# A fused attention and expert kernel on one core: the unused general path made smaller, and the written-out order of the main path replaced

## The chip, the cores and the metric

The kernel runs on one core of a Trainium2 chip. The metric is device time in microseconds, the median of three runs: 174.09 us before the change (173.5 to 175.12). Lower is better. The engines are named as in the profile: PE multiplies matrices, ACT and DVE evict results and do element-wise work, POOL does more element-wise work, SP issues nearly all transfers.

## The reference, cut to what matters

Four batches of 11,456 tokens with 128 channels each. In each batch 32 inducing points attend to all tokens, then every token attends to the 32 results (h). The outcome goes through a router with eight experts, of which each token takes one.

```python
def mab(q, kv):
    s = scale * (q @ kv.transpose(0, 2, 1))
    s = s - s.max(-1, keepdims=True)
    a = np.exp(s)
    a /= a.sum(-1, keepdims=True) + 1e-09
    return a @ kv
h = mab(I, x)
return mab(x, h).astype(np.float32)
...
expert_idx = np.argmax(logits, axis=1)
...
for e in range(E):
    mask = expert_idx == e
    h = np.maximum(x[mask] @ w1[e], 0.0)
    out[mask] = gate_w[mask, None] * (h @ w2[e])
```

## The kernel before, in words

Each batch is cut into six tiles of 1,920 tokens (the last is shorter), 24 tiles in all, numbered g = 0 to 23; tiles 0 to 5 are batch 0, 6 to 11 batch 1, and so on.

The first pass over a tile is `load g` (SP brings 960 KB with channels on partitions into one of ten xT buffers), `s1 g` (scores on PE), `e1 g` (exponentials on ACT), `e1t g` (transposed by DVE) and `h g` (PE accumulates). For `h` the tile is needed with tokens on partitions as well: for the 12 tiles in `LOADED` SP loads that form too (`loadx g`, 960 KB into one of two xD buffers), for the others PE transposes it (`xt g`) and ACT or DVE evicts it (`xe g`). When a batch's six tiles are in, `finish` makes the batch's tables: `hsb`, `hd`, `hdc`, `tab`, then `pick` takes one expert for the whole batch, and `loadw` fetches that expert's two weight matrices (2 x 512 KB), which are read first by `G b` on PE.

The second pass over a tile is `s2 g` (scores against h, the last reader of the tile, after which its xT buffer is free for another load), `e2`, `ud`, `w`, then by pairs of tiles a chain of small steps (`n2`, `ln`, `ex`, `fac`, `den`, `lg`, `el`, `S`, `v`, `gf`), then `F`, `eg`, `out g` on PE, two evictions `oe g.0` and `oe g.1`, and `store g` on SP.

Every such step is one named operation. The string `ORDER` lists all 855 of them; each engine does its own in the order of that string and waits for what they depend on. `BY_DVE` names those done by DVE rather than by their first engine. `Plan.run` walks through `ORDER` with assumed durations (`LATENCY`, `LATE`, `LEAVE` and others are its constants); what it works out decides which buffer of a kind a step takes and where a few dummy matmuls (line 777) are put in. SP's queue goes in order: a load that waits for a free buffer holds back the stores behind it. At most `DEPTH` = 6 loads are under way.

At the end `verdict` (DVE) sums up checks on the shortcuts taken: one int, `ni`, the number of batches for which they did not hold. All five engines read it (line 818, `nc.values_load`) and enter a loop over that many batches (line 821), which computes a batch in a general way, expert by expert. With these inputs `ni` is 0, so the loop's body is never run: each engine loads the value, branches past the body, waits for the outstanding stores, and leaves.

## Time and profile before

| what | before |
|---|---|
| time, median of 3 runs (range) | 174.09 us (173.5 to 175.12) |
| the profiled execution's own time | 173.58 us |
| its span, first to last instruction | 171.8 us |
| PE busy | 154.9 us, 90% of the span |
| DVE, ACT, POOL busy | 123.3, 112.8, 62.7 us |
| moved by DMA | 62.92 MB on SP's queue |
| granted TensorE clock, mean | 0.97 |

Time and span differ by 1.8 us, which lies before the first and after the last instruction. The chain of work that ended last ends at 161.4 us with the verdict; the rest of the span up to 171.8 us is the way out of the program.

### The profile page before, as it was taken

The page shows a single profiled execution, that of the slowest core. Times are in us where ns is not written, and L with a number is a line of the kernel's source. Part 1 is how long each engine was busy: PE and PEld are TensorE (multiplying, and loading weights), DVE is VectorE, ACT ScalarE, POOL GpSimd, SP SyncE. Part 2 cuts the span into 40 slices and gives each one's busy share as a digit, 9 for nine tenths or more (in the row PEclk, how much of TensorE's full clock was granted, in tenths as well). Part 3 has the DMA queues.
Part 4 walks back from the last instruction along what each step waited for, and adds up shares of the span by engine and source line. Part 5 has one row for each costly group of instructions (what it writes and reads, how often), then busy time and mean ns, then how long its engine had stood idle before and what let it go on. Part 6 is the DMA issues. An engine that isn't in the chain of part 4 may idle for free.

```text
span 171.8 us, 5945 instructions
## 1 busy us (share of the span) xinstructions
PE 154.9 (90%) x2383; PEld 84.2 (49%) x2383; DVE 123.3 (72%) x318; ACT 112.8 (66%) x240; POOL 62.7 (37%) x164
## 2 busy tenths in 40 slices
PE   7999999999999999879979999999999999998200
PEld 5686974238955325447257443545733233655100
DVE  0444183887887999668968688898879989988400
ACT  2086923648936798578645975888969899876300
POOL 8400001074126524613133531853650475946000
PEclk9999999999999999999999999999999999999855
DMA  5999999999999589999999999999978999779920
GB/s 171 433 424 411 420 413 419 406 395 423 398 422 415 175 254 422 419 423 424 419 419 418 417 415 420 417 417 420 415 304 334 337 419 396 309 316 391 399 104 8
DMA packets 10865, 63.38 MB, mean 369 GB/s; under 512 B 1352, under 2 KB 1360, under 8 KB 10832
## 3 DMA queue, kind: packets, MB, share of 16 engines
q1 hardware_dynamic: 10656, 62.92, 91.0%
q8 instruction: 21, 0.34, 0.8%
q14 instruction: 12, 0.10, 0.2%
q10 hardware_dynamic: 176, 0.02, 0.1%
HBM read 39.47 MB, written 23.46 MB: 366 GB/s over the span
## 4 chain that ended last, share of the span: by engine, by line
PE 77%; DMA 12%; DVE 3%; issue 1%; SPq 0%; DVEq 0%
PE psum L344 59%; PE psum L448 10%; PE psum L777 7%; DMA w<-in_w 7%; DMA xD<-in_xP 6%; PE psum L416 1%; DVE o L341 1%; PE psum L705 0%; DVE Wp L613 0%; DVE E1T L474 0%; DVE am L595 0%; DVE fl L708 0%; SPq L517 0%; DVE hsb L341 0%; DVE ei L512 0%
## 5 line engine op out<-in xcount | busy, mean ns | idle before, releaser
L341 ACT COPY o<-psum 128x960 f32<-128x960 f32 (+2 forms) x48 | 39.7, 849 | 9.4 <-PE psum L344 8.2
L676 POOL TENSOR_TENSOR E2g<-E,F 128x480 f32<-128x480 f32 (+2 forms) x26 | 26.5, 1031 | 17.5 <-PE psum L344 8.4
L344 PE MATMUL psum<-E2g,K 32*128 32x480 f32 (+2 forms) x232 | 27.1, 542 | 0.5 <-DVE Wp L613 0.2
L344 PE MATMUL psum<-xT,ind 128*32 128x480 f32 x192 | 24.8, 572 | 0.7 <-DMA xT<-in_xT 0.7
L474 DVE STREAM_TRANSPOSE E1T<-E 128x480 f32<-128x480 f32 x24 | 16.0, 670 | 12.1 <-PE psum L344 8.0
L341 ACT COPY xP<-psum 128x1024 f32<-128x1024 f32 (+1 forms) x19 | 18.1, 965 | 8.8 <-PE psum L448 8.8
L448 PEld LDWEIGHTS psum<-ident,xT 128*128 128x128 f32 x180 | 19.8, 142 | 5.3 <-issue 1.6
L344 PE MATMUL psum<-xT,hd 128*32 128x480 f32 x192 | 22.4, 569 | 0.0
L344 PE MATMUL psum<-E,tab 32*32 32x480 f32 x192 | 22.0, 567 | 0.1
L344 PE MATMUL psum<-E,tD 32*32 32x480 f32 x192 | 22.0, 567 | 0.0
L448 PE MATMUL psum<-ident,xT 128*128 128x128 f32 x180 | 21.9, 277 | 0.1
L465 ACT ACTIVATE E<-psum,nb 128x480 f32<-128x480 f32 x24 | 15.8, 659 | 7.7 <-PE psum L344 6.2
L599 ACT ACTIVATE E<-psum,nb 128x480 f32<-128x480 f32 x24 | 14.8, 660 | 5.2 <-DVE nb L419 3.2
L595 DVE TENSOR_REDUCE am<-psum 128x1 f32<-128x480 f32 x24 | 15.3, 648 | 2.0 <-PE psum L344 1.6
L613 POOL TENSOR_TENSOR Wp<-U,E 128x480 f32<-128x480 f32 x9 | 10.9, 1210 | 15.0 <-ACT U L341 14.8
L674 DVE STREAM_TRANSPOSE F<-gf 128x480 f32<-128x480 f32 (+2 forms) x29 | 16.1, 570 | 0.3
L344 PEld LDWEIGHTS psum<-E2g,K 32*128 32x128 f32 x232 | 9.3, 183 | 11.8 <-issue 6.5
L777 PE MATMUL psum<-zero 128*128 128x256 bf16 x82 | 13.1, 306 | 1.3 <-DVE zero L301 1.1
L344 PE MATMUL psum<-xD,E1T 128*32 128x128 f32 x360 | 13.0, 274 | 1.3 <-DMA xD<-in_xP 1.3
L635 DVE TRANSPOSE_TENSOR_REDUCE n<-Wp 128x30 f32<-128x960 f32 x12 | 13.8, 1154 | 0.2
L344 PEld LDWEIGHTS psum<-xD,E1T 128*32 128x32 f32 x360 | 11.0, 110 | 5.7 <-DMA xD<-in_xP 3.2
L344 PE MATMUL psum<-xP,E1T 128*32 128x128 f32 x360 | 13.4, 274 | 0.1
(139 smaller groups left out, 212.2 us busy)
## 6 DMA issues: line engine op xcount, KB each, us to landing
xT<-in_xT SPq DMA_DIRECT2D x19, 960.0 KB, 10.6
out<-o SPq DMA_DIRECT2D x17, 960.0 KB, 9.3
xD<-in_xP SPq DMA_DIRECT2D x12, 960.0 KB, 9.7
w<-in_w SPq DMA_DIRECT2D x8, 512.0 KB, 9.2
xT<-in_xT SPq DMA_DIRECT2D x4, 928.0 KB, 13.5
out<-o SPq DMA_DIRECT2D x5, 512.0 KB, 3.1
out<-o SPq DMA_DIRECT2D x2, 928.0 KB, 5.8
out<-o SPq DMA_DIRECT2D x3, 448.0 KB, 3.5
```

Of the source, the lines that this page charges most:

```text
L341: return nc.scalar.copy(out, in_) if e == "ACT" else ENG[e].tensor_copy(out, in_)
L344: return nc.tensor.matmul(out, lhsT=lhsT, rhs=rhs, start=start, stop=stop)
L448: return [nc.tensor.transpose(ap(tp)[:, (q - q0) // 4, 128 * ((q - q0) % 4):128 * ((q - q0) % 4) + 128], v(q), ident) for q in range(q0, q1)]
L465: return [nc.scalar.activation(ap(e1), ap(ps)[:, :W], AF.Exp, bias=bt.t("nb")[:, 0:1], scale=SCALE, accum_out=bt.t("zk")[:, k:k + 1])]
L474: add(f"e1t {g}", {"DVE": 0.59}, lambda e: [nc.vector.transpose(ap(e1t), ap(e1))], [e1], [e1t])
L595: add(f"am {g}", {"DVE": 0.57}, lambda e, ps=ps, k=k: [v.tensor_reduce(t("am")[:, k:k + 1], ap(ps)[:, :W], AX.X, ALU.max, apply_absolute_v ...
L599: add(f"e2 {g}", {"ACT": 0.56}, lambda e, ps=ps, a=a: [nc.scalar.activation(ap(e2)[:, a], ap(ps)[:, :W], AF.Exp, bias=t("nb")[:, 1:2], sca ...
L613: return [ENG[e].tensor_tensor(ap(wp)[:, a], src(), ap(e2)[:, a], ALU.mult)]
L635: add("n2 " + nm, {"DVE": 1.08}, lambda e: [v.tensor_reduce(fl2(u("n2")), ap(wp).rearrange("p a (q i) -> p (a q) i", i=32), AX.X, ALU.add, ...
L674: add(f"F {nm}", {"DVE": 0.09 + 0.51 * part}, lambda e, a=a, f=f, q0=q0, q1=q1: [v.transpose(ap(f).rearrange("p (q i) -> p q i", i=32)[:, ...
L676: add(f"eg {nm}", {"POOL": 0.06 + 1.15 * part, "DVE": 0.2 + 0.54 * part}, lambda e, a=a, f=f, e2g=e2g, c0=c0, c1=c1: [ENG[e].tensor_tensor ...
L777: fill = [nc.tensor.matmul(psum[:, s, 0:256], lhsT=zero[:, 0:P], rhs=zero, start=True, stop=True) for _ in range(n)]
```

## The change

Three things are changed. First, the body of the general path handles 64 tokens at a time where it handled 358 in three blocks, and its experts are a loop where they were written out eight times: the body's matmuls in the program go from 179 to 28, of which the expert part's go from 128 to 16. Second, `ORDER` and `BY_DVE` are replaced; the operations are the same 855, 32 became 34 of them on DVE, `LOADED` and `W_POOL` stay. Third, `Plan.run` holds every user of a buffer until the buffer is free, where it held only the first; and two of its constants are other (`LATE`, `LEAVE`).

```diff
-ORDER = """load 0.1, ind, load 0.0, load 1, xt 0.1, xe 0.1, s1 0, m1 0, small, en1, xt 0.0, xe 0.0, sha 0, shb 0, s1 1,
+ORDER = """load 0.1, xt 0.1, small, xe 0.1, ind, load 0.0, s1 0, m1 0, xt 0.0, xe 0.0, sha 0, load 1, s1 1, shb 0, shc 0,
...
-    LAND, LATE = 1.2, 0.5
-    LEAVE = 4.0
+    LAND, LATE = 1.2, 1.2
+    LEAVE = 3.0
...
-                    if self.since[b.kind][s] > 0:
-                        t = max(t, self.since[b.kind][s] + wait)
+                    b.open = max(b.open, self.since[b.kind][s])
             for b in o.bufs:
+                if b.open > 0:
+                    t = max(t, b.open + wait)
...
-    GW = 358
-    BLK = ((0, 128), (128, 128), (256, 102))
+    GW = 64
...
-            for e in range(E):
-                nc.sync.dma_start(wr, w1[e])
-                nc.sync.dma_start(w2p, w2[e])
+            with tc.For_i(0, E, 1) as e:
+                nc.sync.dma_start(wr, w1[bass.ds(e, 1)].rearrange("o c f -> (o c) f"))
+                nc.sync.dma_start(w2p, w2[bass.ds(e, 1)].rearrange("o p h c -> (o p) h c"))
+                v.tensor_tensor(r2, place, at_e, ALU.is_equal)
+                v.tensor_scalar_add(at_e, at_e, -1.0)
+                v.tensor_scalar(sq, y, r2, r1, ALU.mult, ALU.mult)
+                nc.tensor.transpose(bank[6][:, 0:GW], sq, ident[:GW, :GW])
+                v.tensor_copy(yg, bank[6][:, 0:GW])
                 for f in range(8):
-                    mm(bank[f % 2][:, :GW], wr[:, P * f:P * f + P], yg[:, e])
-                    nc.scalar.activation(hid, bank[f % 2][:, :GW], AF.Relu)
-                    mm(bank[7][:, :GW], w2p[:, f], hid, start=e == 0 and f == 0, stop=e == E - 1 and f == 7)
-            v.tensor_copy(ot, bank[7][:, :GW])
+                    mm(bank[0][:, :GW], wr[:, P * f:P * f + P], yg)
+                    nc.scalar.activation(hid, bank[0][:, :GW], AF.Relu)
+                    mm(bank[7][:, :GW], w2p[:, f], hid, start=f == 0, stop=f == 7)
+                v.tensor_tensor(ot, ot, bank[7][:, :GW], ALU.add)
```

What the new order does at three places is shown by the instructions as they stand on an engine. `xT_n`, `xD_n` and `xP_n` are buffers of a tile, not tile numbers; the tiles are named in the sentences. Line numbers after the change are one higher.

SP, the first loads, before: tiles 3, 4 and 5, then the second form of tile 3 (`loadx 3`), then tile 6.

```order
L433 DMA xT_68<-in_xT 128x1920
L433 DMA xT_69<-in_xT 128x1920
L433 DMA xT_70<-in_xT 128x1856
L440 DMA xD_78<-in_xP 128x1920
L433 DMA xT_71<-in_xT 128x1920
```

After:

```order
L434 DMA xT_68<-in_xT 128x1920
L434 DMA xT_70<-in_xT 128x1920
L434 DMA xT_69<-in_xT 128x1856
L434 DMA xT_71<-in_xT 128x1920
L441 DMA xD_78<-in_xP 128x1920
```

`load 6` and `loadx 3` have changed places.

SP, in the middle of batch 1, before: loads of tiles 15 and 16, `loadx 13`, `load 17` (which takes the buffer that tile 6 leaves), `store 0`, `load 13`, `store 1`, and the read of the expert's number ahead of `loadw 1`.

```order
L433 DMA xT_68<-in_xT 128x1920
L433 DMA xT_69<-in_xT 128x1920
L440 DMA xD_79<-in_xP 128x1920
L433 DMA xT_71<-in_xT 128x1856
L689 DMA out<-o_97 128x1920
L433 DMA xT_72<-in_xT 128x1920
L689 DMA out<-o_98 128x1920
L517 TENSOR_LOAD ei
```

After: `loadx 13`, `load 13`, `loadx 14`, `load 15`, `store 0`, `load 18` (into the buffer that tile 6 leaves), `store 1`, loads of tiles 16, 20 and 17, the read ahead of `loadw 1`.

```order
L441 DMA xD_78<-in_xP 128x1920
L434 DMA xT_70<-in_xT 128x1920
L441 DMA xD_79<-in_xP 128x1920
L434 DMA xT_69<-in_xT 128x1920
L690 DMA out<-o_97 128x1920
L434 DMA xT_71<-in_xT 128x1920
L690 DMA out<-o_98 128x1920
L434 DMA xT_72<-in_xT 128x1920
L434 DMA xT_73<-in_xT 128x1920
L434 DMA xT_67<-in_xT 128x1856
L518 TENSOR_LOAD ei
```

`store 0` now stands ahead of the load that takes tile 6's buffer, and `load 13` well ahead of it. Between that load and `loadw 1` stand `store 1` and three loads, where `store 0`, `load 13` and `store 1` stood.

PE, where batch 1's weights are first read (`G 1`, the row with `w_149`), before: `s1 13`, `s1 16`, `h 12`, `G 1`, `s2 10`, `s2 11`, `h 13`.

```order
L344 MATMUL psum<-xT_72,ind 32x480 x4
L344 MATMUL psum<-xT_69,ind 32x480 x4
L344 MATMUL psum<-xP_76,E1T_82 32x128 x15
L344 MATMUL psum<-w_149,hd_127 32x256 x4
L344 MATMUL psum<-xT_65,hd_127 32x480 x4
L344 MATMUL psum<-xT_66,hd_127 32x480 x4
L344 MATMUL psum<-xD_79,E1T_82 32x128 x15
```

After, from `s1 13` on, and then from the transposes of tile 17 (23 rows further down) to `h 15`:

```order
L345 MATMUL psum<-xT_70,ind 32x480 x4
L345 MATMUL psum<-xP_75,E1T_83 32x128 x15
L345 MATMUL psum<-xT_65,hd_127 32x480 x4
L345 MATMUL psum<-xT_74,hd_127 32x480 x4
L345 MATMUL psum<-xD_78,E1T_83 32x128 x15
```

```order
L449 MATMUL psum<-ident,xT_67 128x128 x15
L345 MATMUL psum<-w_149,hd_127 32x256 x4
L345 MATMUL psum<-E2g_95,K_122 128x480 x4
L345 MATMUL psum<-xT_67,ind 32x480 x4
L345 MATMUL psum<-xT_71,ind 32x480 x4
L706 MATMUL psum<-ident,chk_123 6x128
L345 MATMUL psum<-tD_129,ones 32x8 x4
L345 MATMUL psum<-ad_164,ones 32x8 x4
L345 MATMUL psum<-xD_78,E1T_83 32x128 x15
```

`G 1` has moved from behind `h 12` to behind the transposes of tile 17, past `s2 11`, `s2 10`, `h 13`, `s1 15`, `h 14`, `out 2`, `ud 10` and `ud 11` (`s1 16` stays ahead of it); and `s1 18`, the transpose for `ck2 0` and the two steps of `md 1` now stand ahead of `h 15` (the last row).

## Rows read from the trace of the kernel before

**Rows 1.** The profile's page: PE's line of the busy times, then the DMA engines' busy share and rate in 40 equal slices of 4.3 us.

```profile
PE 154.9 (90%) x2383; PEld 84.2 (49%) x2383; DVE 123.3 (72%) x318; ACT 112.8 (66%) x240; POOL 62.7 (37%) x164
...
DMA  5999999999999589999999999999978999779920
GB/s 171 433 424 411 420 413 419 406 395 423 398 422 415 175 254 422 419 423 424 419 419 418 417 415 420 417 417 420 415 304 334 337 419 396 309 316 391 399 104 8
```

**Rows 2.** The page's DMA queues: packets, MB, share of the 16 engines' span.

```profile
q1 hardware_dynamic: 10656, 62.92, 91.0%
q8 instruction: 21, 0.34, 0.8%
```

**Rows 3.** Busy time of the engines by stretch (PE, PEld, DVE, ACT, POOL), granted clock, DMA share and rate.

```profile
56.00:64.00 8.00, 8.00 (x116) 2.68 (x114) 7.20 (x23) 6.91 (x17) 3.65 (x6) 1.00 0.69 200
...
124.00:138.00 14.00, 13.78 (x196) 4.64 (x185) 12.26 (x38) 11.35 (x21) 5.70 (x10) 1.00 0.87 333
```

**Rows 4.** PE's own busy time by stretch, with granted clock, DMA share and rate.

```profile
4.90:69.80 64.90, 64.70 (x1043) 1.00 0.98 389
69.80:87.10 17.30, 14.37 (x229) 1.00 1.02 419
87.10:147.80 60.70, 60.27 (x972) 1.00 0.97 392
```

**Rows 5.** PE's instructions in order of time at its three waits for transfers between 64 and 92 us (start, duration; idle time before in brackets): `s1 13` with `s1 16`, `G 1`, `h 15`.

```profile
70.45 1.82 PE L344 MATMUL psum<-xT,ind 128*32 128x480 f32 x16 [0.67 <-DMA xT<-in_xT]
...
74.06 0.64 PE L344 MATMUL psum<-w,hd 128*32 128x256 f32 x8 [0.93 <-DMA w<-in_w]
...
87.08 1.07 PE L344 MATMUL psum<-xD,E1T 128*32 128x128 f32 x30 [1.30 <-DMA xD<-in_xP]
```

**Rows 6.** SP's issues in order of time: `load 17`, `store 0`, `load 13`, `loadw 1`; and, from SP's waits between 40 and 70 us, that of `load 17`.

```profile
58.85 0.33 SPq L433 DMA_DIRECT2D xT<-in_xT  x1
59.22 0.43 SPq L689 DMA_DIRECT2D out<-o  x1
59.75 0.38 SPq L433 DMA_DIRECT2D xT<-in_xT  x1
...
62.57 0.34 SPq L519 DMA_DIRECT2D w<-in_w  x1
...
SPq L433 <- PE psum L344: 9.0, 1, 9.0
```

**Rows 7.** ACT in order of time: the second of the two evictions of tile 0's output (`oe 0.0`).

```profile
55.36 0.97 ACT L341 COPY o<-psum 128x960 f32<-128x960 f32 x1
```

**Rows 8.** The first `loadx` and its user: SP's issue of `loadx 3`, its time to landing (last column), and `h 3` on PE.

```profile
5.72 0.33 SPq L440 DMA_DIRECT2D xD<-in_xP  x1
...
xD<-in_xP SPq DMA_DIRECT2D x1, 960.0 KB, 14.9
...
22.15 1.22 PE L344 MATMUL psum<-xD,E1T 128*32 128x128 f32 x30
```

**Rows 9.** The two issues of `loadw 2` with KB each and time to landing; then SP's issues of `store 6` and `loadw 2` in order of time, and `G 2` on PE.

```profile
w<-in_w SPq DMA_DIRECT2D x2, 512.0 KB, 9.2
...
98.52 0.38 SPq L689 DMA_DIRECT2D out<-o  x1
100.65 0.35 SPq L519 DMA_DIRECT2D w<-in_w  x1
...
111.01 0.62 PE L344 MATMUL psum<-w,hd 128*32 128x256 f32 x8
```

**Rows 10.** The way out, PE's queue: the load of `ni`, and line 821 in the stretches 163.04 to 163.2 and 163.2 to 167.42 and 167.42 to 170.4 us (durations in ns min/median/max, then first and last start).

```profile
L818 PEldq TENSOR_LOAD <-ni x1: 1143/1143/1143, 161.4 to 161.4; - x1
...
L821 PEldq COMPARE_BRANCH  x1: 3770/3770/3770, 163.1 to 163.1; - x1
...
L821 PEldq EVENT_SEMAPHORE  x5: 51/51/51, 167.0 to 167.4; - x5
...
L821 PEldq EVENT_SEMAPHORE  x3: 51/51/51, 167.4 to 170.4; - x3
```

**Rows 11.** Line 821 on the other engines: DVE's second branch, then DVE's, SP's and ACT's semaphores after 163.2 us, and the drains that follow on SP and PE (line 952).

```profile
L821 DVEq COMPARE_BRANCH  x1: 51/51/51, 162.9 to 162.9; - x1
...
L821 DVEq EVENT_SEMAPHORE  x3: 49/49/50, 163.5 to 163.7; - x3
...
L821 SPq EVENT_SEMAPHORE  x12: 17/28/28, 165.3 to 166.5; - x12
L821 ACTq EVENT_SEMAPHORE  x8: 38/38/38, 166.6 to 167.2; - x8
...
L952 SPq DRAIN  x2: 7/10/13, 166.8 to 166.8; - x2
...
L952 PEldq DRAIN  x1: 72/72/72, 170.9 to 170.9; - x1
```

**Rows 12.** The instruction queue q8 in the stretches 163.9 to 165 and 167.5 to 169 us (packets, MB, share of the engines' time).

```profile
q8 instruction: 1, 0.02, 5.7%
...
q8 instruction: 1, 0.02, 5.4%
```

**Rows 13.** DVE at the end: a small step of the verdict, and its last step.

```profile
160.39 0.17 DVE L723 TENSOR_REDUCE fw<-fl 1x1 f32<-1x24 f32 x1
...
161.24 0.13 DVE L726 CAST ni<-fw 1x1 int32<-1x1 f32 x1
```

## The prediction

> **What bounds the kernel now.** I read the page first: PE is busy for 90% of the span, and the DMA engines are full in most of the 40 slices [rows 1]. So two resources are nearly used up. 62.92 MB [rows 2] at the 419 GB/s of a full stretch [rows 4] are 150 us of transfers, and PE has no slack either: 64.7 of 64.9 us busy up to 69.8 us, 60.3 of 60.7 from 87.1 to 147.8 [rows 4]. What a new order can win lies where one of the two stood still.

> PE stood still between 69.8 and 87.1 us: 14.37 of 17.30 us [rows 4]. The rows show three waits, all for transfers: 0.67 us at `s1 13` for its tile, 0.93 at `G 1` for the expert's weights, 1.30 at `h 15` for the tile's second form [rows 5]. That is 2.90 us. The transfers were late because the DMA engines had run dry before: from 56 to 64 us they moved 200 GB/s [rows 3], so 8 x (1 - 200/419) = 4.2 us were lost. The queue's rows name the reason: SP held `load 17` for 9.0 us, since its buffer is only free after `s2 6`, and behind it stood `store 0` (whose data were evicted by 56.3 us [rows 7]) and `load 13`; both left at 59.2 and 59.8 [rows 6]. A second thin stretch, 124 to 138 us at 333 GB/s, loses 2.9 us [rows 3], but there PE is busy and the stores wait for its results, so it is no cause.

> The other part is the end. The verdict is ready at 161.4 us [rows 13] and the span ends at 171.8: 10 us in which nothing is computed. Every engine loads the flag (1.14 us) and branches past the general path's body. DVE branches at 162.9 and does its next semaphores at 163.5 [rows 11], 0.6 us later, though 120 of its rows are jumped over. SP's last semaphores start at 165.3, when the last store has landed, and SP drains at 166.8 [rows 11]. PE is the one that is late: its branch takes 3.77 us, then come five semaphores at 0.1 us each, then only three between 167.4 and 170.4 [rows 10]; it drains at 170.9 [rows 11]. In both gaps the instruction queue q8 brings one packet [rows 12]. A q8 packet is 16 KB (0.34 MB in 21), and 4,766 instructions of PE [rows 1] in 21 packets make about 230 a packet, so q8 feeds PE. I read the two gaps as waits for instructions that had not been brought.

> **The exit, costed.** In the body before, 179 matmul calls are jumped over. One call is up to four of PE's instructions: `h 15` has 15 calls and 30 matmuls [rows 5], and as many weight loads as matmuls are counted [rows 1]. That makes up to 716 instructions, about three packets; after, 28 calls make up to 112, half a packet, and some 80 for loops and semaphores come on top in either. A jump that stays in the packet under way or the next one should cost what DVE's did. PE would then branch at 163.1, go on at about 163.7, meet the store's landing at 165.3 and drain some 1.1 us later (eight semaphores at 0.1 and a branch), ahead of SP at 166.8. From PE's drain to the end of the span are 0.85 us, so the end is 166.8 + 0.85 = 167.65 instead of 171.75: **-4.1 us**. ACT shows the same stall (its semaphores come at 166.6 [rows 11]); with ACT's left as it is the end would be 167.4 + 0.8 and the gain 3.5. The lower bound is nothing: the gaps stay.

> [...]

> The new order puts more of the verdict's small steps behind the last eviction: five instead of one, of 0.13 and 0.17 us [rows 13], say 0.2 with what lies between, so the flag comes some 0.8 us later against the last store. It is read by 162.2 + 1.2, still ahead of the landing at 165.3, which hides it: nothing. Without that cover (if PE still stalls) it costs the 0.8.

> **The order, costed.** `G 1` moves behind nine PE steps of about 1 us each (`h 15` took 1.07, two `s1` 1.82 [rows 5]), so it stands at about 82 us where the weights came at 74.0 [rows 5]. In the queue `loadw 1` has one more transfer ahead than before behind tile 6's buffer; even 2.3 us later (960 KB at 419 GB/s) it is in time: -0.93. `load 13` now waits for the fifth buffer that `s2` frees, not for the eighth behind `load 17`, and is done long before 69.8: -0.67. `h 15` has `s1 18`, `ck2 0`, `md 1` and `G 1` ahead in addition, 1.9 us of work that is only moved, and in the queue `load 19` goes behind: -1.30. For DMA, `store 0` fills 2.3 us of the dry stretch once it is evicted at about 56.5; since it flows only a while after that I count 1.7 us of 4.2 recovered. The next deadline is then `G 2`: `loadw 2` landed at 100.65 + 9.2 = 109.9 for a use at 111.0 [rows 9], 1.1 us of margin; with PE 2.1 earlier and the transfers 1.7 it is 0.7. So the lead holds to 124 us, and behind that DMA has its 2.9 us of slack.

> One step is worse. `load 6` now goes ahead of `loadx 3`, which landed at 5.72 + 14.9 = 20.6 for an `h 3` that began at 22.15 [rows 8]. One transfer of 960 KB later is 22.9: PE, which has nothing idle there, waits **+0.8** (0 if the queue is less strict, 1.2 at most). The other exchanges among the steps of PE leave sets of work in front of each table step as they were; the evictions that go from ACT to DVE and back weigh 32 against 34, on engines that are 66 and 72% busy [rows 1]: nothing. `small` now stands ahead of `ind` in ACT's queue, both needed only behind the first tile: nothing, 0.4 at most. At the end half an `eg` of tile 22 goes from POOL to DVE, beside its other half, but `F 23.1` goes behind two evictions: between -1 and +1, I take 0. The corrected planner issues no instruction itself; it acts through the buffers chosen and six more dummy matmuls, which fill waits: nothing.

> Sum for the order: -2.9 + 0.8 = **-2.1 us**, between -3.9 (no wait at `h 3`, the end 1 us better) and +1.8 (no wait goes, `h 3` costs 0.8, the end 1 us worse). Sum of both: 173.58 - 4.1 - 2.1 = 167.4 for the profiled execution; the median of the runs is 0.5 above it, so **167.9 us**.

> **The rivals.** *The order wins nothing*: the waits only move, because the DMA engines are nearly as full as PE and each transfer moved up pushes another back. For it: the slices from 64 to 124 us stay near 420 GB/s whatever stands in the queue [rows 1]. Against it: 4.2 us of dryness are there to be used. 174.09 - 4.1 = 170.0, up to 171.8 with the order's upper end.

> *The exit does not shrink*: PE's stall is not set by the length of the jump, or the target still lies in a packet that was not brought. For it: the second gap, which comes five instructions after the first and may be a matter of where a packet ends. Both gaps left: 174.09 - 2.1 + 0.8 = 172.8. Only the second gone (2.8 us): 170.0. [...]

> *Slower*: `store 6` now stands in SP's queue ahead of `loadx 19`, `load 22` and `loadw 2`; before, it left at 98.5, two issues behind [rows 9]. If its evictions are held up, the weights for `G 2` are late and PE, which goes in order, stops at 111 us. The margin of 0.7 us is gone when `store 6` leaves more than 0.7 us later than its share of the queue allows; to be slower in the end PE must stand there longer than 6.2 us, and by 1% longer than 7.9, which gives 175.9 and more. For it: everything behind is held in one queue. Against it: where the rows show a store late it is the queue that holds it, not its evictions (tile 0: evicted by 56.3, issued at 59.2 [rows 6, 7]).

> **How the numbers follow.** Forecast (both parts, 166 to 169.9): 0.57. Order wins nothing (170 to 171.8): 0.16. Exit not shrunk: 0.16, half of it at 170.0, half at 172.8. Slower, 175.9: 0.05. Still faster than 166, through waits that I don't see: 0.06. The range reaches from the sum of the better ends, 174.1 - 4.1 - 3.9 = 166.1, less 0.6 for the spread of the runs (173.5 against 174.09), to the order's worse end with the exit's gain, 171.8: **165.5 to 171.8**, which leaves out half of the exit rival and the slower one, and a little below. This kernel's runs tell about 1%, 1.74 us, from no change. Faster (under 172.3): 0.57 + 0.16 + 0.08 + 0.06, some of it just at the edge, 0.85; within 1%: 0.10; slower: 0.05.

> **What would show it.** In the profile after: PE's branch on the loop's line takes 0.1 to 0.6 us, and PE's drain comes ahead of SP's; the end lies about 2.4 us behind the landing of the last store, not 6.5. PE has no idle time for w or xT near 70 to 75 us and none for xD near 85; there is one for xD of about 0.8 at 22 us. The slices at 56 to 64 us show well over 200 GB/s. The last store is issued about 2 us earlier than at 161.4. The prediction is wrong if a branch of over 2 us remains, or if the three waits come back under other names, such as w at `G 2` near 109 us.

## The result, and the profile after

The kernel after takes 168.19 us (median of 4 runs, 166.87 to 168.9) where the kernel before, timed beside it, takes 174.61: a ratio of 0.963, 95% interval 0.955 to 0.971. Forecast was 167.9 us. The profiled execution took 168.47 us with a span of 166.7 us; before, 173.58 and 171.8.

The page of the kernel after, PE's line and the DMA engines in 40 slices of 4.2 us, beside [rows 1]; then four stretches (PE's busy time, granted clock, DMA share, rate), beside [rows 3, 4]; then all of PE's waits of 0.2 us and more in the span, beside [rows 5].

```profile
PE 156.2 (94%) x2389; PEld 84.0 (50%) x2389; DVE 126.2 (76%) x322; ACT 112.2 (67%) x236; POOL 61.6 (37%) x162
...
DMA  5999999999999999999999999999996999889891
GB/s 162 429 424 422 413 419 411 402 340 411 417 415 408 404 315 361 417 420 423 411 413 421 386 410 420 415 424 415 424 417 278 344 383 387 330 314 379 340 403 73
```

```profile
56.00:64.00 8.00, 8.00 (x116) 1.00 0.96 331
64.00:72.00 8.00, 7.90 (x103) 1.00 1.01 417
...
4.90:69.80 64.90, 63.31 (x1027) 1.00 1.01 400
69.80:87.10 17.30, 17.30 (x282) 1.00 1.02 416
```

```profile
PE psum L345 <- DMA ind<-in_indT: 1.1, 1, 1.1
PE psum L778 <- DVE zero L302: 1.1, 1, 1.1
PE psum L345 <- DMA xD<-in_xP: 0.5, 2, 0.3
PE psum L345 <- ACT o L342: 0.2, 1, 0.2
PE psum L778 <- ACT o L342: 0.2, 1, 0.2
```

The dry stretch is largely filled (331 GB/s for 200, where a full stretch has 419), the three waits of [rows 5] are gone, and PE works through all 17.30 us in which it had worked 14.37. Two waits for transfers are new: one for `ind` at the start, and short ones for xD, of 0.25 us at `h 3` and as much at another tile. (The wait for `zero` ahead of the first matmuls is in both kernels.)

The way out, beside [rows 10, 11] (the loop stands on line 821 in both kernels): PE's load of `ni`, its second branch, its eight semaphores, its third branch and its drain; SP's last semaphores; and SP's last issue of a store.

```profile
L819 PEldq TENSOR_LOAD <-ni x1: 1148/1148/1148, 161.6 to 161.6; - x1
L821 PEldq COMPARE_BRANCH  x1: 187/187/187, 163.3 to 163.3; - x1
L821 PEldq EVENT_SEMAPHORE  x8: 51/51/51, 163.5 to 165.5; - x8
L821 PEldq COMPARE_BRANCH  x1: 176/176/176, 165.6 to 165.6; - x1
L951 PEldq DRAIN  x1: 8/8/8, 165.9 to 165.9; - x1
...
L821 SPq EVENT_SEMAPHORE  x4: 28/28/28, 165.1 to 165.3; - x4
...
160.82 0.33 SPq L690 DMA_DIRECT2D out<-o  x1
```

PE's branch takes 0.19 us for 3.77, and its semaphores wait for the store at 165.1, not for instructions (from 161.95 us on the queue q8 brings none). But the last store is issued at 160.82 us, only 0.57 earlier than the 161.39 before.

### The profile page after: what moved, and what is told of

Its sections match the earlier page's. It is cut to its first block, busy times and chain, and to the rows that moved or that the text cites. A ratio compares the mean times of both kernels' runs of the same rounds, so it can differ in the third digit from the quotient of the medians.

```text
span 166.7 us, 5953 instructions
## 1 busy us (share of the span) xinstructions
PE 156.2 (94%) x2389; PEld 84.0 (50%) x2389; DVE 126.2 (76%) x322; ACT 112.2 (67%) x236; POOL 61.6 (37%) x162
## 3 DMA queue, kind: packets, MB, share of 16 engines
q1 hardware_dynamic: 10656, 62.92, 94.1%
## 4 chain that ended last, share of the span: by engine, by line
PE 69%; DMA 19%; ACT 6%; issue 1%; DVE 1%; SPq 0%
PE psum L345 57%; DMA xD<-in_xP 15%; PE psum L449 6%; PE psum L778 5%; DMA xT<-in_xT 4%; ACT o L342 4%; PE psum L417 1%; ACT s L646 1%; SPq L432 0%; ACT E L600 0%; ACT gf L663 0%; PE psum L706 0%; DVE o L342 0%; ACT s L647 0%; ACT ex L656 0%
## 5 line engine op out<-in xcount | busy, mean ns | idle before, releaser
L677 POOL TENSOR_TENSOR E2g<-E,F 128x480 f32<-128x480 f32 (+2 forms) x24 | 24.8, 1045 | 23.7 <-DVE F L675 13.5
L342 ACT COPY xP<-psum 128x1024 f32<-128x1024 f32 (+1 forms) x19 | 17.6, 961 | 10.3 <-PE psum L449 10.2
L675 DVE STREAM_TRANSPOSE F<-gf 128x480 f32<-128x480 f32 (+2 forms) x29 | 15.6, 565 | 0.1
L778 PE MATMUL psum<-zero 128*128 128x256 bf16 x88 | 13.6, 302 | 1.3 <-DVE zero L302 1.1
```

The costliest lines, as they stand in the source:

```text
L342: return nc.scalar.copy(out, in_) if e == "ACT" else ENG[e].tensor_copy(out, in_)
L675: add(f"F {nm}", {"DVE": 0.09 + 0.51 * part}, lambda e, a=a, f=f, q0=q0, q1=q1: [v.transpose(ap(f).rearrange("p (q i) -> p q i", i=32)[:, ...
L677: add(f"eg {nm}", {"POOL": 0.06 + 1.15 * part, "DVE": 0.2 + 0.54 * part}, lambda e, a=a, f=f, e2g=e2g, c0=c0, c1=c1: [ENG[e].tensor_tensor ...
L778: fill = [nc.tensor.matmul(psum[:, s, 0:256], lhsT=zero[:, 0:P], rhs=zero, start=True, stop=True) for _ in range(n)]
```

## Experiments

### Each half alone

`e1`: before, with the general path of after. `e2`: after, with the general path of before.

> The kernel before with only the general path's body made small; order, engines and planner as before. Theory (the exit is set by the length of the jump): PE's branch on the loop's line falls from 3.77 us to under 0.6, the second gap of 2.8 us is gone, the span ends about 2.2 to 2.6 us behind the last store's issue plus landing instead of 6.5, the last store is issued at 161.4 as before: 4.1 to 4.5 us less, some 169.5 to 170. Rival (the gain of the change is the order's): within 1 us of before. Rival (the second gap comes from where a packet ends): the first gap gone, 2.8 left, gain 1.3 to 1.7 only.

> The changed kernel with the large general path of before: new order, engines and planner alone. If order and exit add up: the last store issued at about 160.8, PE's branch again 3.8 us and perhaps a second gap; as the flag is ready 0.8 us later against the last store than before, the gain of 0.6 at the last store is lost at the exit: 174 to 174.6, no change within 1%. As the prediction had it (order 2.1 us better, 0.8 lost): 172.8. Rival (both halves needed together, the exit's gain only appears with the new order): under 171.

Measured: the exit alone 169.3 us (ratio 0.969, 0.963 to 0.974), the order alone 170.42 us (0.979, 0.971 to 0.986). By the ratios one takes 5.5 us off, the other 3.7: together 9.2, where the whole change takes off 6.5. They share something. First the exit alone, PE's branch and semaphores; then the order alone, with the long body, the same two.

```profile
L820 PEldq COMPARE_BRANCH  x1: 310/310/310, 163.8 to 163.8; - x1
...
L820 PEldq EVENT_SEMAPHORE  x8: 51/51/51, 164.2 to 166.5; - x8
```

```profile
L822 PEldq COMPARE_BRANCH  x1: 3888/3888/3888, 162.2 to 162.2; - x1
...
L822 PEldq EVENT_SEMAPHORE  x8: 51/51/51, 166.2 to 166.9; - x8
```

With the exit alone the branch takes 0.31 us, and the semaphores wait for the last store, up to 166.1 us, together with those of the other four engines (the last of each starts at 166.3 to 166.5 us), and no longer for instructions, as forecast. With the order alone the branch stalls as before (3.89 us), but the eight semaphores follow each other at 0.1 us: the second gap of [rows 10], 2.8 us, is gone though the body is the old one. What is common to both halves is that gap. (The order alone ended under 171 us, where its last rival had it, but not for that rival's reason.)

### What the second gap hangs on

The new order runs 14 instructions of PE more ahead of the exit (six more dummy matmuls among them: 4,868 records for 4,854). So the place of the jump's target within a packet of instructions is another. Two kernels move that place by instructions that are never run:

```diff
-        nc.tensor.transpose(bank[0][:, 0:M], hs, ident[:M, :M])
+        for _ in range(5):      # e6, in before; e7: 122, in the order-alone kernel
+            nc.tensor.transpose(bank[0][:, 0:M], hs, ident[:M, :M])
```

> The kernel before, with one transpose of the general path written five times instead of once: eight more instructions of PE in a body that is never run; nothing that is run is changed. Question: what PE's second gap in the exit (167.4 to 170.3 us before, 2.8 us) hangs on, and why the order alone took it away. Theory A: the jump's target lies five instructions ahead of the end of a packet of 256 instructions, so PE runs five semaphores and has to wait for the next packet; eight instructions further on the target lies at the start of a packet, one wait is left, and the kernel is 2.8 us faster than before: 171.9 us against 174.7, with PE's branch still at 3.7 to 3.9 us and all eight semaphores 0.1 us apart. Theory B: the second gap comes from something else (the length of the jump, a second taken branch): both gaps stay, 174.7 us, within 0.6.

> The new order with the old general path (as in the order-alone kernel), and one transpose of that path written 122 times: 242 more instructions of PE in a body that is never run. In that kernel the target of the jump lay 14 instructions further than before, and the second gap was gone; 14 and 242 are 256. Theory A (place in a packet of 256): the second gap is back, and the time is that of the order alone plus 2.8 us: 173.2 us, which would leave the order a gain of 1.5 us beside an unchanged exit. Theory B (the order removes the second gap in another way, by when the engines arrive): no second gap, 170.4 us.

Measured: 171.78 us (ratio 0.985, 0.981 to 0.989) and 173.49 us (0.993, 0.989 to 0.996). PE's queue, first `e6`, then `e7`:

```profile
L821 PEldq COMPARE_BRANCH  x1: 4015/4015/4015, 163.2 to 163.2; - x1
L821 PEldq EVENT_SEMAPHORE  x8: 51/51/51, 167.3 to 168.1; - x8
```

```profile
L822 PEldq COMPARE_BRANCH  x1: 4792/4792/4792, 163.1 to 163.1; - x1
L822 PEldq EVENT_SEMAPHORE  x5: 51/51/51, 168.0 to 168.4; - x5
...
L822 PEldq EVENT_SEMAPHORE  x3: 51/51/51, 171.0 to 171.2; - x3
```

Eight instructions that nobody runs make the kernel before 2.7 us faster by the ratio; 242 bring the gap back after exactly five semaphores, as in [rows 10]. So the gap comes back after 256 instructions, which with the prediction's count of some 230 for each packet of q8 makes a packet of 256, by estimate; and it comes where the target lies just ahead of a packet's end. With the gap in both kernels (`e7` against before) the order is worth 1.2 us of the median (0.6 to 1.9). With it in neither, it is worth 1.0 us, whether the body is short (0.963 against 0.969) or long (`e2` against `e6`, 0.979 against 0.985); these two differences are not clear of noise by themselves. The other 2.5 us of the order-alone kernel were a shift by 14 instructions. One thing is open: the profiled execution of `e7`, 0.8 us slower than its median, has a branch of 4.79 us for 3.77, with two packets of q8 under way at once (from 163.57 and 164.08 us), so its exit was not quite that of before, and the 1.2 us may be too low.

In steps, then: the second gap 2.7 us (before to `e6`), the first stall 2.8 (`e6` to `e1`), the order 1.0 (`e1` to after).

### How long the unused body may be

```diff
-            with tc.For_i(0, E, 1) as e:
+            with tc.For_i(0, E, 4) as e0:      # e11; e12: 8
+                for d in range(4):
+                    e = e0 + d
```

> The kernel after, its general path with four experts written out per turn of the loop: about 385 instructions of PE are jumped over instead of 184 (before: 726). Theory: what is left of the packet under way and the next packet of 256 have been brought when PE branches; in the kernel after a packet had just begun, so up to some 500 instructions cost nothing: branch 0.1 to 0.3 us, span 166.7. Rival: only the packet under way counts, 250 at most: PE's branch takes 3.8 us, the span is 169.

> As the kernel with four experts per turn, with eight: about 653 instructions of PE are jumped over. Theory: beyond the two packets, so the branch takes 3.7 to 3.9 us; the target lies some 190 instructions into a packet, so there is no second gap; the span is 2.3 us longer than after's, 169.0. Rival (the jump's length isn't what counts, the 179 matmuls with their blocks of 358 tokens are): no stall, 166.7.

Measured, one execution each: 171.45 us (span 169.7) and 170.36 (168.6). For `e11` PE's second branch, then SP's last semaphores; for `e12` PE's second branch, PE's semaphores, SP's last semaphores:

```profile
L821 PEldq COMPARE_BRANCH  x1: 412/412/412, 163.5 to 163.5; - x1
...
L821 SPq EVENT_SEMAPHORE  x8: 27/28/28, 168.2 to 168.6; - x8
```

```profile
L821 PEldq COMPARE_BRANCH  x1: 3888/3888/3888, 162.2 to 162.2; - x1
L821 PEldq EVENT_SEMAPHORE  x8: 51/51/51, 166.1 to 166.9; - x8
...
L821 SPq EVENT_SEMAPHORE  x8: 28/28/28, 167.1 to 167.5; - x8
```

For PE both branches came out as expected: 385 instructions cost 0.41 us, 653 cost 3.89. Where between the two the wait sets in, no run shows. The time of `e11` missed, because of an engine that the expectation left out: SP resumes 2.6 us after its branch at 165.6 (in after 0.5 us), and is the last to drain in both kernels. SP's body has grown as well; that this is the reason is argued, not tested apart. So the span of `e12`, 168.6 for 169.0, is SP's end too and no second sign for PE's 3.89 us. PE may not be the only engine that loses this way: in the kernel before, ACT branched at 162.8 us and did its next semaphores at 166.6 [rows 11].

### What the new order is worth, and why

Since the start and the exit vary, the order is best read from the transfers: the time at which the last full stretch of the DMA engines ends. (Ten or more data packets of queue q1 under way.) Each row is one execution.

| kernel | order | last store issued | full rate ends | last data packet | span ends |
|---|---|---|---|---|---|
| before | old | 161.39 | 164.23 | 164.45 | 171.8 |
| e1 | old | 162.17 | 165.03 | 165.66 | 167.6 |
| e6 | old | 161.47 | 164.35 | 166.07 | 169.2 |
| after | new | 160.82 | 163.19 | 164.59 | 166.7 |
| e2 | new | 159.79 | 162.13 | 164.01 | 168.0 |
| e7 | new | 160.57 | 162.92 | 163.27 | 172.5 |
| e11 | new | 161.11 | 163.49 | 164.91 | 169.7 |
| e12 | new | 159.74 | 162.08 | 163.59 | 168.6 |

Old order 164.5 on average, new order 162.8: 1.8 us earlier (1.6 with `e13` below, at 163.75). Two single moves, each in the kernel before, were to show which of them brings it.

```diff
-s1 16, e1 16, h 12, zk 1, G 1, eg 5, s2 10
+s1 16, e1 16, h 12, zk 1, eg 5, s2 10
...
-n2 10, mq 1, loadx 15, v 6, out 5, s1 17
+n2 10, loadx 15, v 6, G 1, GT 1, gs 1, out 5, ..., s1 17
```

> The kernel before with G 1 alone moved to where the new order has it, ahead of out 5 (and behind it the few small steps that need its result). Theory of the prediction: the 0.93 us that PE waited for the expert's weights go and nothing comes in their place, so out 6 on PE begins at about 91.1 us instead of 92.05, the wait at h 15 stays at 1.3. Rival (the transfers set the pace, waits only move): the wait at h 15 grows from 1.30 to about 2.2 us and out 6 begins at 92.0 as before. Compared from s1 0 on, since the start varies from run to run.

Measured, one execution: 176.74 us. PE's waits from 64 to 92 us, `h 15` itself, and PE's busy time and granted clock around it:

```profile
PE psum L342 <- DMA xD<-in_xP: 2.2, 1, 2.2
PE psum L342 <- DMA xT<-in_xT: 0.7, 1, 0.7
...
89.00 1.91 PE L342 MATMUL psum<-xD,E1T 128*32 128x128 f32 x30 [2.19 <-DMA xD<-in_xP]
...
86.80:89.00 2.20, 0.01 (x2) 1.00 1.01 415
89.00:92.60 3.60, 3.60 (x39) 0.53 1.02 427
```

The 0.93 us at `G 1` are gone, and the wait at `h 15` is 2.2 us as the rival said: the wait moved. It also came out dearer. Behind 2.2 us of idleness the granted clock is 0.53 for 3.6 us (behind the 1.30 us before it stayed at 1.00), and `h 15` took 1.91 us for 1.07. So `out 6` began not as before, as the rival had it, but 1.6 us later counted from `s1 16` (23.2 for 21.6). The rest of the loss came with an execution that was 1.9 us late by `s1 16` already.

```diff
-loadx 13, ln 4, ..., load 17, ..., store 0, ..., load 13
+loadx 13, ln 4, ..., store 0, load 13, load 17
```

> The kernel before with store 0 and load 13 alone moved ahead of load 17 in the order; G 1 stays where it was. Theory: the dry stretch of the DMA engines (56 to 64 us, 200 GB/s) is what makes the three transfers late; with store 0 in it the rate there rises to 280 GB/s or more, and the three waits on PE, 2.90 us in all, shrink by 1.5 to 2.3 us, so that out 6 begins at about 90 us instead of 92.05. Rival (the waits come from where the steps stand on PE, not from the queue): they stay at 2.5 to 2.9 us, and out 6 begins at 91.7 to 92.1.

Measured, one execution: the rates of the two stretches, PE's waits from 64 to 92 us, and SP's issues of `store 0` and `load 13`.

```profile
56.00:64.00 8.00, 7.36 (x112) 1.00 0.80 304
64.00:72.00 8.00, 8.00 (x107) 1.00 1.00 345
...
PE psum L342 <- DMA xD<-in_xP: 1.1, 1, 1.1
PE psum L342 <- DMA w<-in_w: 0.6, 1, 0.6
...
58.26 0.35 SPq L687 DMA_DIRECT2D out<-o  x1
61.63 0.33 SPq L431 DMA_DIRECT2D xT<-in_xT  x1
```

The rate rose as expected, but the next stretch fell from 420 to 345: SP now held `load 13` until 61.6 us. Over both stretches 5.19 MB moved, 4.96 before, 5.98 in the kernel after. `out 6` began 85.6 us behind `s1 0`, as before (92.05 - 6.43); the waits shrank only because PE itself ran later, some of it by a wait of 0.74 us at 56.7 us without a named releaser, of which the next section says more. So neither move is the cause by itself. What the new order does as a whole is to bring 1.0 MB more, 2.4 us of full rate, through these 16 us; which of its loads is decisive stays open, and that the waits go because of it is argued from the traces, not tested by a run. (Its 171.76 us are no gain of the stores: the second gap is absent, eight semaphores of PE follow each other from 168.0 us; by `e6` and `e7` that is put down to five more instructions of PE.)

### The start and `h 3`

`e3`: after, `ind` ahead of `small`. `e4`: in addition `loadx 3` ahead of `load 6`, as in before.

> The changed kernel with one thing undone: ACT issues the load of ind ahead of the two small loads, as before. Theory (PE is full from the first tile on, so a late start stays late to the end): the wait of 1.1 us of PE at s1 0 for ind goes, s1 0 starts at 6.4 instead of 7.3, the wait at h 3 for xD grows from 0.3 to 0.8 or more, and tile 1's table steps, out 0 and s2 6 come 0.4 to 0.9 us earlier; time 0.3 to 0.9 us under the changed kernel's, about 167.5. Rival (transfers bound from 64 us on, so the head start is lost): s2 6 earlier, the last store not.

> As the run with ind first, and loadx 3 ahead of load 6 again, as before. Theory: no wait of PE for xD at h 3 either, which then starts at 22.1 as before; out 0 at 52.8 and s2 6 at 57.3; time 0.9 to 1.4 us under the changed kernel's, 166.8 to 167.3. Rival (transfers bound): the last store is issued at 160.8 as in the changed kernel, with longer idle time of PE in the middle or the end.

Measured: 167.71 us (0.957, 0.949 to 0.965) and 167.08 (0.958, 0.951 to 0.965), neither to be told from after's 0.963. PE at the start in after (the first tile's transposes, then `s1 0`), then the same two in `e3`:

```profile
4.78 0.93 PE L449 MATMUL psum<-ident,xT 128*128 128x128 f32 x7
...
7.34 1.01 PE L345 MATMUL psum<-xT,ind 128*32 128x480 f32 x8 [1.09 <-DMA ind<-in_indT]
```

```profile
4.87 1.70 PE L447 MATMUL psum<-ident,xT 128*128 128x128 f32 x7
...
7.16 1.01 PE L343 MATMUL psum<-xT,ind 128*32 128x480 f32 x8
```

The wait for `ind` is gone in `e3`, but its transposes took 1.70 us, and `s1 0` came only 0.18 us earlier; the wait at `h 3` stayed at 0.24 us, where the expectation had it grow. The time goes with TensorE's clock: the trace's records of the full clock begin at 6.67 us in `e3` and at 4.66 us in after, and ahead of them one transpose follows another at 0.213 us, behind them at 0.109. All 14 traces agree: in seven the records begin by 5.2 us and the seven transposes take 0.93 to 1.08 us, in the other seven at 6.4 to 6.9 us and they take 1.61 to 1.70. PE began its dummy matmuls 1.05 to 1.07 us after the start in all of them. Over all runs `s1 0` began between 5.9 and 8.1 us whatever the order. In `e4` `h 3` follows `s1 5` without a wait (0.71 us, 1.33 in after), but at `G 0` PE is where it was in after (42.35 against 42.30): what is won early is lost again by then, some of it in a wait of 0.33 us, up to 41.39 us, for which the rows name no releaser. The packets of q8 point to one: of eight such waits on PE in the 14 traces (0.2 to 0.9 us; in `e1`, `e4`, `e8`, `e9`, `e11` and `e13` one each, in `e10` two) each ends 1.2 to 1.6 us behind the end of a packet (here 39.93 us), and so do the stalls of the exit (before: packets up to 165.46 and 168.89 us, PE on at 166.95 and 170.25), but for one of 2.3 us in `e7`. So PE most likely waited for instructions here too, without any branch. The time of `e4` lies in the range expected, yet the last store was issued at 160.56 us, only 0.26 earlier than in after, near to what the rival had.

### The tail

`e8`: `e4`, with `F 23.1` and its `eg` ahead of the evictions of tile 22, and the checks behind those of tile 23.

> The kernel after with ind ahead of small, loadx 3 ahead of load 6, and another order of the tail: F 23.1 and its eg ahead of the evictions of tile 22, the checks' last steps behind the evictions of tile 23. If the lead of the new order is lost at the end because F 23.1 waits behind two evictions on DVE, out 23.1 comes 0.7 to 1.4 us earlier against out 23.0 and the last store with it, and the median is 166.2 us, 1.9 below the kernel after and 0.8 below the kernel with the first two edits alone (167.1). If the tail is bound by the evictions and the stores' transfers themselves, it stays at 167.1; if the checks, now last, delay the flag beyond the landing of the last store, it is up to 1 us slower than that.

Measured: 168.25 us (0.963, 0.959 to 0.967), no gain. SP's last issue of a store, the DMA engines' rate (last column) in `e8`, and the instruction packet between 162.75 and 163.6 us:

```profile
159.37 0.39 SPq L688 DMA_DIRECT2D out<-o  x1
...
156.00:162.00 6.00, 3.07 (x37) 1.23 (x29) 4.18 (x19) 2.53 (x5) 0.30 (x1) 1.00 1.01 405
162.00:163.00 1.00, 0.00 (x0) 0.00 (x0) 0.00 (x0) 0.00 (x0) 0.00 (x0) 0.50 0.69 256
...
q8 instruction: 1, 0.02, 6.5%
```

The last store left 1.45 us earlier than in after, into DMA engines that were full until 162.7 us. Up to that point the tail is bound by transfers, not by the step that comes last: from the start of `out 21` on PE to the end of the full rate are 11.0 to 11.1 us in all 14 traces, whatever the order of the tail, such as before (153.18, 164.23), after (152.15, 163.19), `e2` (151.11, 162.13) and `e8` (151.62, 162.70).

### What the last packets wait for

In `e8` the instruction packet came at 162.77 us, and the last few data packets came behind it, from 164.06 to 164.47. In after one came at 161.05, and some ten data packets followed one by one, 0.13 us apart, as from one engine, up to 164.59, 1.4 us after the end of the full rate. `e13` is after with eight dummy matmuls fewer ahead of `out 22.1`.

> The kernel after with eight dummy matmuls fewer, of those that fill PE's wait ahead of out 22.1 near 153 us; nothing else. It is to test what the last packets of the stores wait for. In the traces so far the last data packet comes 0.2 to 0.65 us behind the point where most DMA engines fall idle when no instruction packet of PE (16 KB, 0.9 us) is brought in the last 4 us of the stores, and 1.45 to 1.9 us behind it when one is (after: one at 161.05 us, 1.45 us). Theory: the packet occupies one of the 16 DMA engines and delays its share of the last stores. With 16 instructions of PE fewer ahead of the exit, PE enters the next packet only with the exit's jump, so the packet is brought at about 163.3 us, when the stores are through: the last data packet then comes 0.2 to 0.7 us behind, and the median falls from 168.2 to about 167.1 us. Rival (the late packets belong to the stores themselves, whatever else the queue brings): 1.4 us stay, 168.2 us. The target of the jump stays within the packets that have been brought, so PE's branch should take 0.2 to 0.4 us as in the kernel after.

The queues in after, first from 161 to 162 us, then behind the full rate, from 163.2 to 164.6; in `e13` from 163.86 to 164.9, and PE's branch (packets, MB, share):

```profile
q8 instruction: 1, 0.02, 5.5%
...
q1 hardware_dynamic: 21, 0.04, 8.2%
```

```profile
q8 instruction: 1, 0.02, 6.3%
...
q1 hardware_dynamic: 1, 0.00, 0.0%
...
L822 PEldq COMPARE_BRANCH  x1: 188/188/188, 163.1 to 163.1; - x1
```

Measured: in the trace as the theory has it. The packet comes at 163.88, the full rate ends at 163.75, the last data packet is at 163.88 (0.1 us behind, for 1.4), and the branch takes 0.19 us. The time missed: the median is 168.34 us (0.964, 0.958 to 0.969), not 167.1. That is no gain over after's 0.963, though the intervals would hide one of 1 us, and run-to-run changes elsewhere are as large (`out 21` came 0.55 us later in this execution). What holds up the packets is shown in the traces; what it costs the median is not.

## Why the prediction came out

The total was right, 167.9 for 168.19, but partly by luck: two terms missed by 1 us and more in opposite directions.

**The bounds** were read rightly: two nearly full resources, and gain only where both stood still, in the dry stretch and in the exit.

**The exit, forecast -4.1, was under-sized**: -5.5 us alone (4.5 to 6.5). Its mechanism (waits for packets of instructions, a body short enough to stay in those already brought) held in `e1`, `e11` and `e12`: branches of 0.31 and 0.41 us with the shorter bodies, 3.89 with the longest. That a jump is cheap as far as the packet under way and the next one was the author's estimate and not shown as a limit; the runs have 0.41 us at 385 instructions and 3.89 at 653. The forecast put the end 2.35 us behind SP's landing of the last store (165.3 and 167.65), with all of PE's eight semaphores still to come; in after it is 1.6 us behind (165.1 and 166.7), since PE has run three of them before. Counted from the last data packet, before needs 7.3 us and after 2.1.

**That the second gap is a matter of where a packet ends** stood among the rivals as a doubt against the forecast. It is right as a mechanism, and I did not see that the order, too, moves the target. The short body has no such gap; but by the counts, 726 and 184, it moves the target by 542 instructions, which is 30 within a packet, and no run tells whether it escapes by being short or only by that shift.

**The order, forecast -2.1, was over-sized**: -1.0 to -1.2 us of the median. By its terms, from PE's records in one execution each of before and after: the stretch from `h 3` to `out 8`, in which the three waits lie, gives what was forecast for them, 3.07 us for 2.9 (from 1.61 us behind to 1.46 ahead). `h 3` costs 0.6 us for 0.8. The step that failed is "`small` ahead of `ind`: nothing, 0.4 at most": `s1 0` began 0.91 us later, with 1.09 us of waiting for `ind`; though `e3` shows that without this wait the start can lose as much to a late clock. From `out 8` to `out 21`, 0.4 us of the lead went. The tail, put at 0, is 0: in before and after the full rate ends 11.0 us behind `out 21`. And 1.2 us went where the forecast had no term: the last data packets. In these two executions nothing of the order's gain was left at that point, since the last data packet comes 0.1 us later than before (164.59 and 164.45); the 1.0 to 1.2 us are those of the medians.

**The reasons for the three waits were only partly right.** I costed each by its own step (`G 1` later, `load 13` and `store 0` earlier). `e9` and `e10` do not bear that out: alone, the first moves the wait to `h 15`, the second moves the dry stretch. It was the rival's mechanism, transfers that set the pace, that decided the wait in `e9`; the order as a whole wins against it, most likely since it fills the dry stretch.

**The other rivals**: `G 2` has no wait in after, so `store 6` held nothing up. Of the marks that the prediction named, the branch, the three waits and the 331 GB/s came out; PE's drain is still behind SP's (165.9 and 165.5), since both wait for the same landing; the last store left 0.6 us earlier, not 2.

## What to carry to other kernels

Code that never runs had a price on the way past it: PE's branch took 0.41 us past 385 instructions and 3.89 past 653. Keep such code short, look at every engine (ACT in before went on 3.8 us after its branch), and look for a branch of several us (3.77 in before) and for a hole in an even row of semaphores (2.8 us behind the fifth). When two halves of a change add up to more than the whole, look for a cost that both remove. Removing a wait on a full resource can move it (in `e9` the 0.93 us at `G 1` went, and the wait at `h 15` grew from 1.30 to 2.2); look at the resource's own dry stretches and at the bytes moved through them, and don't repair a tail that ends in full transfers (in `e8` the last store left 1.45 us earlier than in after, and the ratio was 0.963 in both).
